# Attention with two feed-forward layers on one core: the half-filled query tile weighed by the full array, and the cosine's turn count written by ScalarE

## The chip, the cores and the metric

The kernel runs on one core of a Trainium2 chip. The metric is the device time of one execution in microseconds (us). The core has TensorE (PE; PEld is its weight load), VectorE (DVE), ScalarE (ACT), GpSimd (POOL) and SyncE (SP), whose queue here issues all transfers.

## What is computed

Attention over 4 batches and 8 heads with queries pooled in pairs (576 queries, 1152 keys, 64 wide), then two feed-forward layers over the 2304 rows; the first has the activation h·cos(h), the second silu.

```python
q_pool = q.reshape(B, H, S // factor, factor, D).mean(axis=3)
scores = scale * np.matmul(q_pool, k.transpose(0, 1, 3, 2))
attn = np.exp(scores - np.max(scores, axis=-1, keepdims=True))
attn = attn / (np.sum(attn, axis=-1, keepdims=True) + 1e-09)
x = np.matmul(attn, v)                    # heads side by side: 2304 x 512
h = x @ moe_w_in                          # 512 x 2048
x = (h * np.cos(h)) @ moe_w_out           # 2048 x 512
h = x @ moe2_w_in
out = (h * (1.0 / (1.0 + np.exp(-h)))) @ moe2_w_out
```

## The kernel before

All matmuls run in float16 pairs (a high and a low part of each number), three products for one.

**Attention.** Heads are taken in 16 pairs (4 batches, 4 pairs each). A pair has 576 queries per head, which make four full tiles of 128 queries for either head and one shared tile: 64 queries of the first head in its upper half, 64 of the second in its lower half. So there are nine tiles a pair and 144 in all. A tile goes through `tile_scores` (TensorE into PSUM), `tile_exp` (VectorE scales and finds the maximum, L409 and L414; ScalarE takes the exponential, L417), `tile_hi` (ScalarE, L423), `tile_lo` (GpSimd, L428, then a transposing transfer into `hlT`) and, four tiles later, `tile_pv` (L442), where the transposed weights are the stationary operand and the values move: 27 matmuls of 65 or 64 columns. For the shared tile `tile_pv` runs 27 matmuls on the first 64 stationary columns with the first head's values, and then 27 on the other 64 columns with the second head's values, each into its own 64 partitions of one slot of `pv`. `group_end` divides up to five tiles at a time on VectorE (L451 to L461).

**First layer.** The rows go through in nine blocks of 256 (two a batch, and one of all the shared tiles' rows). A block has 16 units `g1_unit` (L518, 12 matmuls of 256 columns each); two units fill a PSUM tile `h`, of which there are two. `g1_evac` (L531) copies two units to `hk`, scaled to turns. Every four units make a group of 128x1024: VectorE adds a quarter and a large constant (L543), takes the constant and `hk` off again (L544), which leaves the rounded turn count less the turns, ScalarE takes the sine (L550), VectorE multiplies (L553) and rounds to float16 (L558), GpSimd forms the low part (L559), and TensorE uses the result in `g2_unit1` (L578). The buffer `tt` of a group has two copies, shared with the block's result `y32` (L585 to L590), which is written to DRAM. There are 36 groups.

**Order.** First-layer units are handed out between the attention tiles (`share`), and a scheduler with priorities sets each engine's order when the program is built; the first layer's matmuls, the scores and the weighing of values therefore come interleaved in TensorE's queue, often one by one. The second layer's weights are decoded on VectorE, ScalarE and GpSimd (L206 to L240) after the last attention pair is loaded. The second layer (L518, L599) follows when the first is done.

Of the kernel before, what the change touches and what calls it, by code (L numbers as in the profile page):

```python
# [11 lines left out]
F32 = mybir.dt.float32  # L12
F16 = mybir.dt.float16
I32 = mybir.dt.int32
AF = mybir.ActivationFunctionType
ALU = mybir.AluOpType
# [5 lines left out]
MAGIC = 12582912.0  # L22
# [14 lines left out]
NB_HK, NB_TT, NB_G, SIN_N = 2, 2, 2, 2  # L37
# [3 lines left out]
GT = 5  # L41
# [3 lines left out]
def attention_moe_moe_kernel(ctx, tc, q, k, v, w_in1, w_out1, w_in2, w_out2, out):  # L45
# [3 lines left out]
    nc = tc.nc  # L49
    B, H, S, D = q.shape  # L50
# [6 lines left out]
    NT = SQ // 128  # L57
# [3 lines left out]
    const = ctx.enter_context(tc.tile_pool(name="const", bufs=1))  # L61
    wpool = ctx.enter_context(tc.tile_pool(name="w1", bufs=1))
    small = ctx.enter_context(tc.tile_pool(name="small", bufs=2))
# [3 lines left out]

    mean = const.tile([128, 128], F32, name="mean")
    halfpi = const.tile([128, 1], F32, name="halfpi")

    def make_consts():
        nc.vector.memset(mean, 2.0**-7)
        nc.vector.memset(halfpi, math.pi / 2)

    GW = 256

# [36 lines left out]
    @contextmanager  # L113
    def ahead(n):

        at_ = tc.cur_priority
        tc.cur_priority = at_ - n
        yield
        tc.cur_priority = at_ + (tc.cur_priority - (at_ - n))
# [147 lines left out]
    def att_pools(stack):  # L267
        at = Weights()
        at.p = stack.enter_context(tc.tile_pool(name="att", bufs=2, side="right", reuse_waits="tile"))
        at.src_stack = ExitStack()  # L270
        at.src = at.src_stack.enter_context(tc.tile_pool(name="src", bufs=2, side="right", reuse_waits="tile"))
        at.ps_s = stack.enter_context(tc.tile_pool(name="ps_s", bufs=1, space=PSUM, side="right"))
        at.ps_v = stack.enter_context(tc.tile_pool(name="ps_v", bufs=1, space=PSUM, side="right"))
        return at
# [102 lines left out]
    def tile_scores(at, P, t):  # L377


        T = Pair()  # L380
        T.P, T.t = P, t

        parts = [(0, 512), (512, S)]
        T.sp = [(a, z, at.ps_s.tile([128, z - a], F32, tag="sp%d" % a, name="sp")) for a, z in parts]
        if t < 2 * NT:
            kT = P.kT[t // NT]
            for a, z, sp in T.sp:
                for o, n in segs:
                    for e in range(2 if a <= o < z else 0):
                        nc.tensor.matmul(  # L390
                            sp[:, o - a:o - a + n], P.qT[e][:, t, :], kT[:, o:o + n], start=(e == 0), stop=(e == 1)
                        )
        else:
            for a, z, sp in T.sp:
                for o, n in segs:
                    for e in range(2 if a <= o < z else 0):
                        for i in range(2):
                            nc.tensor.matmul(
                                sp[i * 64:(i + 1) * 64, o - a:o - a + n], P.qT[e][:, t, i * 64:(i + 1) * 64],
                                P.kT[i][:, o:o + n], start=(e == 0), stop=(e == 1),  # L400
                            )
        return T
# [31 lines left out]
    def tile_pv(at, T):  # L434
        P, t, G = T.P, T.t, T.G
        if T.gi == 0:
            G.pv = at.ps_v.tile([128, GT, D + 1], F32, tag="pv", name="pv")
        hs = [(slice(0, 128), t // NT)] if t < 2 * NT else [(slice(0, 64), 0), (slice(64, 128), 1)]
        for r, i in hs:
            for c in range(KC):  # L440
                for e, z, n in ((0, 0, D + 1), (0, 1, D), (1, 0, D + 1)):
                    nc.tensor.matmul(  # L442
                        G.pv[r, T.gi, 0:n], T.hlT[:, e, c, r], P.vt[i][:, c, z, 0:n],
                        start=(c == 0 and e == 0 and z == 0), stop=(c == KC - 1 and e == 1),
                        skip_group_check=True,
                    )

    def group_end(at, G, n, dsts):

        den = small.tile([128, GT, 1], F32, tag="den", name="den", bufs=2)  # L450
        nc.vector.tensor_scalar(  # L451
            out=den[:, 0:n], in0=G.pv[:, 0:n, D:D + 1], scalar1=1e-9 * 2.0**PSH, scalar2=G.P.s[:, 2:3],
            op0=ALU.add, op1=ALU.mult,
        )
        nc.vector.reciprocal(den[:, 0:n], den[:, 0:n])
        for o, shape, dst in dsts:
            k = math.prod(shape)
            src, d = G.pv[:, o:o + k, 0:D], den[:, o:o + k].to_broadcast([128, k, D])
            if len(shape) == 2:
                src, d = (x.rearrange("p (t a) d -> p t a d", a=shape[1]) for x in (src, d))  # L460
            nc.vector.tensor_tensor(out=dst, in0=src, in1=d, op=ALU.mult)  # L461
# [62 lines left out]
    def g1_evac(mp, w, blk, f, first):  # L524
        if f % 2 == 0:
            return
        g = f * w.npc // NF
        if f % 4 == 1:
            blk.hk = mp.p.tile([128, 4, GW], F32, tag="hk", name="hk", bufs=NB_HK)
        o = blk.hk[:, (f % 4) - 1:(f % 4) + 1, :]  # L530
        nc.scalar.activation(  # L531
            out=o, in_=blk.hp, func=AF.Copy if first else AF.Silu, scale=blk.c.a[:, g:g + 1]
        )

    def g_cos_begin(mp, blk):

        G = Block()
        G.hk, G.K = blk.hk, blk.c.k
        G.gh = mp.p.tile([128, 4, GW], F16, tag="gh", name="gh", bufs=NB_G)
        G.gl = mp.p.tile([128, 4, GW], F16, tag="gl", name="gl", bufs=NB_G)  # L540
        blk.g.append((G.gh, G.gl))
        G.t = t = mp.p.tile([128, 4, GW], F32, tag="tt", name="tt", bufs=NB_TT)
        nc.vector.tensor_scalar(out=t, in0=G.hk, scalar1=0.25, scalar2=MAGIC, op0=ALU.add, op1=ALU.add)  # L543
        nc.vector.scalar_tensor_tensor(out=t, in0=t, scalar=MAGIC, in1=G.hk, op0=ALU.subtract, op1=ALU.subtract)  # L544
        return G

    def g_cos_end(groups):
# [68 lines left out]
    if True:  # L616
# [3 lines left out]
        xrem = wpool.tile([128, B, NP * D], F32, name="xrem")  # L620

        att_stack = ExitStack()
        at = att_pools(att_stack)
        wst_stack = ExitStack()
        wst = wst_stack.enter_context(tc.tile_pool(name="wst", bufs=1, reuse_waits="tile"))
        moe_stack = ExitStack()
        make_consts()

        state = Weights()
# [13 lines left out]
        def finish(g):  # L643
            while g in bg:
                advance()
# [45 lines left out]
        P = {}  # L691
# [36 lines left out]
        def x_of(b, i):  # L728
            if (b, i) not in x32:
                if (b - 1, i) in xgens:  # L730
                    finish(xgens[b - 1, i])
                x32[b, i] = wpool.tile([128, 2, DM], F32, tag="x32_%d" % i, name="x32")
            return x32[b, i]

        def block_done(b, i):
            if state.mp is None:
                finish(wg)
                wst_stack.close()
                state.mp = moe_pools(moe_stack)
            xgens[b, i] = block_steps(b, i)  # L740
            bg.append(xgens[b, i])

        def drain_pv():
            T = inflight.pop(0)
            G = T.G
            with ahead(P_PV):
                tile_pv(at, T)
            if T.gi < len(G.tiles) - 1:
                return
            b, j = T.P.b, T.P.j  # L750
            dsts = []
            if j < NP - 1:
                h = j + (G.tiles[0] // NT) * NP
                for i in range(2):
                    dsts.append((2 * i, (2,), x_of(b, i)[:, :, h * D:(h + 1) * D]))
            else:
                x = x_of(b, G.tiles[0] % NT // 2).rearrange("p t (a h d) -> p t a h d", a=2, d=D)
                dsts.append((0, (2, 2), x[:, :, :, j, :]))
            if G.tiles[-1] == 2 * NT:
                dsts.append((len(G.tiles) - 1, (1,), xrem[:, b:b + 1, j * D:(j + 1) * D]))  # L760
            group_end(at, G, len(G.tiles), dsts)
            if j == NP - 1:
                left[b] = left.get(b, set(range(2 * NT))) - set(G.tiles)
                for i in range(2):
                    if (b, i) not in gone and all(t % NT // 2 != i for t in left[b]):
                        gone.add((b, i))
                        block_done(b, i)
# [3 lines left out]
        for n, (b, j) in enumerate(pairs):  # L771
# [7 lines left out]
            for o in range(0, len(seq), GT):  # L779
                G = Pair()  # L780
# [9 lines left out]
            for idx, (G, gi, t) in enumerate(order):  # L790
                with ahead(P_SC):
                    T = tile_scores(at, P[n], t)
# [14 lines left out]
        while inflight:  # L807
            drain_pv()
            share(1)
# [23 lines left out]
        for i in range(2):  # L833
            T = wpool.tile([128, B, 2, 128], F16, tag="x32_%d" % i, name="xrT")
# [68 lines left out]
        for n in range(NB):  # L903
            nyb = y_load(n + 1) if n + 1 < NB else None
            gen = y_split(nyb) if nyb else None
            for f in range(NF):
# [7 lines left out]
                if len(pend) > 8:  # L914
                    blk, ff, nn = pend.pop(0)
# [43 lines left out]
```

## Time and profile before

| | us |
|---|---|
| median of three runs | 1435.6 (1434.48 to 1436.16) |
| profiled execution, its own time | 1439.78 |
| its span | 1438.0 |
| PE busy in the span | 1189.1 (83%) |
| DVE busy | 992.8 (69%) |
| ACT busy | 736.7 (51%) |
| POOL busy | 561.3 (39%) |

Busy time is an average over stages that differ: up to about 300 us there is attention alone with the decoding of the first layer's weights, up to about 888 us attention and first layer together, up to about 1037 us the rest of the first layer with the decoding of the second layer's weights, and from there on the second layer. In the rows, `128*64` is the part of the array that a matmul uses (rows by columns), `x22` is a count, and what stands behind `<-` in brackets is what ended an idle time.

### The profile page before, as it was taken

What the parts mean: (1) busy time and instruction counts of PE and PEld (TensorE: products, weight loads), DVE (VectorE), ACT (ScalarE), POOL (GpSimd) and SP (SyncE); (2) the same over time, 40 slices, a digit from 0 to 9 for tenths busy, and PEclk for the clock granted to TensorE, in tenths of its full rate; (3) what the DMA queues carried; (4) which work ended last, traced back from release to release, by engine and by line L of the source; (5) the groups of instructions that cost most, each with busy time, mean ns of one, the idle gap of its engine ahead of it and who ended that gap; (6) DMA issues with size and microseconds to landing.
All of it is one profiled execution on the core that took longest, in us unless ns stands there. A gap on an engine that the chain in (4) does not pass through costs nothing. (4 is left out here: it accounts for less than half of the span.)

```text
span 1438.0 us, 27552 instructions
## 1 busy us (share of the span) xinstructions
PE 1189.1 (83%) x11460; PEld 870.2 (61%) x11460; DVE 992.8 (69%) x1840; ACT 736.7 (51%) x763; POOL 561.3 (39%) x264
## 2 busy tenths in 40 slices
PE   1455365779988877998979989898899999999998
PEld 0233244566766655676656768777786666666665
DVE  7999987598787867987798895999833222323212
ACT  3676486477667667776667665546511111111110
POOL 1578375454556474656645552545410000000000
PEclk9986568798999998999999999989899999999999
DMA  7799889986799999997997965434210000000001
GB/s 230 191 232 199 206 161 187 207 159 111 153 210 164 198 204 185 202 162 161 182 188 144 222 102 107 123 113 132 74 60 30 15 16 30 30 30 15 16 1 30
DMA packets 493085, 186.34 MB, mean 130 GB/s; under 512 B 433056, under 2 KB 467872, under 8 KB 492960
## 3 DMA queue, kind: packets, MB, share of 16 engines
q1 hardware_dynamic: 492960, 184.59, 62.5%
q8 instruction: 89, 1.46, 0.4%
q14 instruction: 36, 0.29, 0.1%
HBM read 66.58 MB, written 9.44 MB: 53 GB/s over the span
## 5 line engine op out<-in xcount | busy, mean ns | idle before, releaser
L428 POOL TENSOR_TENSOR hl<-sc,hl 128x1152 f16<-128x1152 f32 x144 | 368.0, 2564 | 221.9 <-ACT hl L423 132.6
L442 PE MATMUL pv<-vt,hlT 128*128 128x65 f16 (+3 forms) x4320 | 253.5, 206 | 61.6 <-DMA hlT<-hl 45.2
L442 PEld LDWEIGHTS <-hlT 128*128 128x128 f16 (+1 forms) x4320 | 208.2, 108 | 119.0 <-DMA hlT<-hl 57.3
L518 PEld LDWEIGHTS <-ih 128*128 128x128 f16 x2304 | 226.4, 99 | 75.1 <-issue 14.9
L390 PE MATMUL sp<-kT,qT 128*128 128x512 f16 (+1 forms) x768 | 193.0, 366 | 95.1 <-DVE sc L409 77.7
L409 DVE TENSOR_SCALAR_CACHE_REDUCE sc<-sp,psu 128x512 f32<-128x512 f32 (+1 forms) x288 | 229.9, 808 | 52.1 <-PE sp L390 43.3
L531 ACT ACTIVATE hk<-h,ca 128x512 f32<-128x512 f32 x144 | 98.2, 683 | 326.8 <-PE h L518 326.8
L417 ACT ACTIVATE sc<-sc,nb 128x1152 f32<-128x1152 f32 x144 | 179.8, 1251 | 152.2 <-DVE nb L414 129.0
L518 PE MATMUL h<-ys,ih 128*128 128x256 f16 x1152 | 197.4, 274 | 2.9 <-ACT hk L531 2.9
L518 PE MATMUL h<-xT,ih 128*128 128x256 f16 x1024 | 190.6, 278 | 7.9 <-DVE pu__2739 L98 3.4
L423 ACT ACTIVATE hl<-sc 128x1152 f16<-128x1152 f32 x144 | 165.6, 1157 | 19.3 <-DMA hlT<-hl 11.7
L566 DVE TENSOR_SCALAR gh<-hk,ck 128x1024 f16<-128x1024 f32 x36 | 27.0, 751 | 206.9 <-PE o L599 194.2
L390 PEld LDWEIGHTS <-qT 128*128 128x128 f16 x768 | 76.3, 108 | 153.3 <-issue 112.3
L578 PE MATMUL y<-gh,oh 128*128 128x256 f16 x576 | 162.4, 282 | 4.2 <-ACT y L587 4.2
L578 PE MATMUL y<-gl,oh 128*128 128x256 f16 x576 | 162.2, 282 | 0.0
L578 PE MATMUL y<-gh,ol 128*128 128x256 f16 x576 | 162.0, 281 | 0.0
L518 PE MATMUL h<-ys,il 128*128 128x256 f16 x576 | 157.6, 274 | 0.0
L518 PE MATMUL h<-xT,il 128*128 128x256 f16 x512 | 142.7, 279 | 0.0
L559 POOL TENSOR_TENSOR gl<-tt,gh 128x1024 f16<-128x1024 f32 x36 | 87.6, 2434 | 112.7 <-DVE gh L558 82.3
L578 PEld LDWEIGHTS <-oh 128*128 128x128 f16 x1152 | 115.2, 101 | 23.8 <-issue 4.7
L518 PEld LDWEIGHTS <-il 128*128 128x128 f16 x1152 | 114.2, 99 | 18.9 <-issue 1.4
L599 PE MATMUL o<-ol,gh 128*128 128x512 f16 x288 | 109.1, 379 | 0.0
(279 smaller groups left out, 1776.6 us busy)
## 6 DMA issues: line engine op xcount, KB each, us to landing
wst<-in_moe_w_in_dram SPq DMA_DIRECT2D x16, 1024.0 KB, 6.1
wst<-in_moe_w_out_dram SPq DMA_DIRECT2D x16, 1024.0 KB, 6.1
stk<-in_k_dram SPq DMA_DIRECT2D x32, 288.0 KB, 4.1
stv<-in_v_dram SPq DMA_DIRECT2D x32, 288.0 KB, 4.1
stq<-in_q_dram SPq DMA_DIRECT2D x32, 256.0 KB, 3.2
ydr<-y SPq DMA_DIRECT2D x9, 512.0 KB, 2.6
y32b<-ydr SPq DMA_DIRECT2D x9, 512.0 KB, 3.2
out_dram<-osb SPq DMA_DIRECT2D x16, 256.0 KB, 2.1
```

What stands on the lines that cost most here:

```text
L390: nc.tensor.matmul(sp[:, o - a:o - a + n], P.qT[e][:, t, :], kT[:, o:o + n], start=(e == 0), stop=(e == 1))
L409: nc.vector.tensor_scalar(out=T.sc[:, a:z], in0=sp, scalar1=T.P.su, scalar2=None, op0=ALU.mult, op1=ALU.min, accum_out=mx[:, x:x + 1],)
L417: nc.scalar.activation(out=T.sc, in_=T.sc, func=AF.Exp, scale=-1.0, bias=nb)
L423: nc.scalar.activation(out=hi, in_=T.sc, func=AF.Copy)
L428: nc.gpsimd.tensor_tensor(out=T.hl[:, 1, :], in0=T.sc, in1=T.hl[:, 0, :], op=ALU.subtract)
L442: nc.tensor.matmul(G.pv[r, T.gi, 0:n], T.hlT[:, e, c, r], P.vt[i][:, c, z, 0:n], start=(c == 0 and e == 0 and z == 0), stop=(c == KC - 1 a ...
L518: nc.tensor.matmul(hp, wt[:, c, f * 128:(f + 1) * 128], xt(c), start=(i == 0), stop=(i == 3 * NC - 1), skip_group_check=True,)
L531: nc.scalar.activation(out=o, in_=blk.hp, func=AF.Copy if first else AF.Silu, scale=blk.c.a[:, g:g + 1])
L559: nc.gpsimd.tensor_tensor(out=G.gl, in0=t, in1=gh, op=ALU.subtract)
L566: nc.vector.tensor_scalar(out=gh, in0=hk, scalar1=blk.c.k, scalar2=None, op0=ALU.mult)
L578: nc.tensor.matmul(blk.y[:, oc, :], wt[:, f, oc * 128:(oc + 1) * 128], gt[:, f % 4, :], start=(f == 0 and e == 0 and oc % 2 == 0), stop=(f ...
L599: nc.tensor.matmul(blk.y[i], gt[:, f % 4, i * 128:(i + 1) * 128], wt[:, f, :], start=(f == 0 and e == 0), stop=(f == NF - 1 and e == 2),)
```

## The change

Two things are changed. The shared tile's weights are loaded whole (128 columns) in `tile_pv`, once with the first head's values and once with the second's, into two slots of `pv` of 128 partitions each, of which only the fitting half is divided and kept; `pv` and `den` get a sixth slot, and `group_end` writes the two halves apart. And in the first layer ScalarE reads each PSUM tile `h` a second time and writes turns plus a quarter into `tt` as 32-bit integers, with a bias of 0.25 from a 128x1 tile; VectorE's pass L543 goes, and L544 becomes a subtraction of `hk` from the integers. `tt` is now taken when the group's first two units are evacuated, where it was taken after its fourth.

```diff
     def tile_pv(at, T):
...
-        hs = [(slice(0, 128), t // NT)] if t < 2 * NT else [(slice(0, 64), 0), (slice(64, 128), 1)]
-        for r, i in hs:
+        for x, i in enumerate([t // NT] if t < 2 * NT else [0, 1]):
             for c in range(KC):
                 for e, z, n in ((0, 0, D + 1), (0, 1, D), (1, 0, D + 1)):
                     nc.tensor.matmul(
-                        G.pv[r, T.gi, 0:n], T.hlT[:, e, c, r], P.vt[i][:, c, z, 0:n],
+                        G.pv[:, T.gi + x, 0:n], T.hlT[:, e, c], P.vt[i][:, c, z, 0:n],
...
     def g1_evac(mp, w, blk, f, first):
...
             blk.hk = mp.p.tile([128, 4, GW], F32, tag="hk", name="hk", bufs=NB_HK)
+            if first:
+                blk.tt = mp.p.tile([128, 4, GW], F32, tag="tt", name="tt", bufs=NB_TT)
...
+        if first:
+            nc.scalar.activation(
+                out=blk.tt.bitcast(I32)[:, (f % 4) - 1:(f % 4) + 1, :], in_=blk.hp, func=AF.Identity,
+                scale=blk.c.a[:, g:g + 1], bias=quarter,
+            )
...
-        G.t = t = mp.p.tile([128, 4, GW], F32, tag="tt", name="tt", bufs=NB_TT)
-        nc.vector.tensor_scalar(out=t, in0=G.hk, scalar1=0.25, scalar2=MAGIC, op0=ALU.add, op1=ALU.add)
-        nc.vector.scalar_tensor_tensor(out=t, in0=t, scalar=MAGIC, in1=G.hk, op0=ALU.subtract, op1=ALU.subtract)
+        G.t = t = blk.tt
+        nc.vector.tensor_tensor(out=t, in0=t.bitcast(I32), in1=G.hk, op=ALU.subtract)
...
             if G.tiles[-1] == 2 * NT:
-                dsts.append((len(G.tiles) - 1, (1,), xrem[:, b:b + 1, j * D:(j + 1) * D]))
+                for i in range(2):
+                    r = slice(i * 64, (i + 1) * 64)
+                    dsts.append((len(G.tiles) - 1 + i, (1,), xrem[r, b:b + 1, j * D:(j + 1) * D], r))
```

The first place where the issued order matters is TensorE, in the weighing of a shared tile of the second batch (`hlT_3679` before, `hlT_3692` after). Before:

```order
L442 LDWEIGHTS hlT_3679
L442 MATMUL pv_3701<-vt_3030,hlT_3679 64x64
L578 LDWEIGHTS ol1_84
L578 MATMUL y_3121<-gh_3354,ol1_84 128x256
L442 LDWEIGHTS hlT_3679
L442 MATMUL pv_3701<-vt_3030,hlT_3679 64x65
L578 LDWEIGHTS oh1_83
L578 MATMUL y_3121<-gh_3354,oh1_83 128x256
```

And with the change:

```order
L443 LDWEIGHTS hlT_3692
L443 MATMUL pv_3713<-vt_3040,hlT_3692 128x65
L586 LDWEIGHTS ol1_85
L586 MATMUL y_3130<-gh_3367,ol1_85 128x256
L443 LDWEIGHTS hlT_3692
L443 MATMUL pv_3713<-vt_3040,hlT_3692 128x65
L586 LDWEIGHTS oh1_84
L586 MATMUL y_3130<-gh_3367,oh1_84 128x256
```

The one-by-one interleaving with the first layer stays; the weighing matmuls have 128 output partitions where they had 64. Over the program the shared tiles' weighing stood in 160 runs between other matmuls and now stands in 142.

The second place is ScalarE at the end of a first-layer block, after the attention (the group of `hk_12096` before, of `hk_12141` after; `y32` is the previous block's result). Before:

```order
L531 ACTIVATE hk_12096<-h_12045,ca_11466 128x512
L550 ACTIVATE tt_12017<-tt_12017,halfpi_73 128x1024
L238 ACTIVATE ih2_11530<-wst_11629,si2_112 128x4x256
L587 ACTIVATE y32_12037<-y_11281,cy_8678 128x256 x3
L206 ACTIVATE wt_11875<-wst_11775 128x1024
L587 ACTIVATE y32_12037<-y_11281,cy_8678 128x256
L831 ACTIVATE xnr_11523<-xrem_94,srem_11498 128x1024
L531 ACTIVATE hk_12096<-h_12117,ca_11466 128x512
```

And with the change:

```order
L535 ACTIVATE hk_12141<-h_12090,ca_11509 128x512
L595 ACTIVATE y32_12082<-y_11322,cy_8708 128x256 x4
L240 ACTIVATE ih2_11573<-wst_11671,si2_114 128x4x256
L841 ACTIVATE xnr_11566<-xrem_95,srem_11541 128x1024
L535 ACTIVATE hk_12141<-h_12164,ca_11509 128x512
L241 ACTIVATE wst_11671<-wst_11671,si2_114 128x1024
L208 ACTIVATE wt_11919<-wst_11818 128x1024
L539 ACTIVATE tt_12142<-h_12090,quarter_74,ca_11509 128x512
L539 ACTIVATE tt_12142<-h_12164,quarter_74,ca_11509 128x512
```

Both PSUM tiles `h` of the group are now read a second time at the end of this piece, behind the previous block's `y32` and two weight steps; before, each was free after its one reading.

## Rows read from the trace of the kernel before

**Rows 1.** Windows: span us, busy us of each engine (instructions), PEclk, DMA share, GB/s.
```profile
300.00:888.00 588.00, 505.80 (x5971) 383.57 (x5969) 479.54 (x948) 403.13 (x404) 328.47 (x155) 0.95 0.93 172
888.00:1037.00 149.00, 132.04 (x1112) 112.80 (x1110) 139.98 (x198) 85.38 (x94) 68.23 (x26) 0.93 0.37 107
1037.00:1438.00 401.00, 395.84 (x2776) 271.61 (x2774) 115.39 (x160) 64.03 (x91) 6.37 (x3) 0.99 0.08 26
```
**Rows 2.** Chain that ended last, in order of time: start us, us, what.
```profile
1013.57 2.38 DVE tt L543
...
1040.88 4.15 PE y L578 x38
```
**Rows 3.** Waits of TensorE and VectorE, 300 to 888 us: us in total, times, longest.
```profile
PE sp L390 <- DVE sc L409: 45.8, 33, 4.3
...
DVE sc L409 <- PE sp L390: 31.8, 30, 4.5
DVE den L451 <- PE pv L442: 14.7, 4, 5.4
```
**Rows 4.** Timeline of TensorE, a shared tile: start us, us, engine, line, operation, count.
```profile
816.07 0.22 PE L442 MATMUL pv<-vt,hlT 128*64 128x65 f16 x1
816.22 0.28 PE L578 MATMUL y<-gh,ol 128*128 128x256 f16 x1
816.43 0.22 PE L442 MATMUL pv<-vt,hlT 128*64 128x65 f16 x1
```
**Rows 5.** Timeline of TensorE, a full tile in the same interleaving.
```profile
601.60 0.19 PE L442 MATMUL pv<-vt,hlT 128*128 128x64 f16 x1
601.62 0.28 PE L578 MATMUL y<-gl,oh 128*128 128x256 f16 x1
601.74 0.19 PE L442 MATMUL pv<-vt,hlT 128*128 128x65 f16 x1
```
**Rows 6.** Timeline of TensorE: first and last half-width run of 300 to 888 us.
```profile
317.90 0.41 PE L442 MATMUL pv<-vt,hlT 128*64 128x65 f16 x7
...
865.15 1.46 PE L442 MATMUL pv<-vt,hlT 128*64 128x65 f16 x43
```
**Rows 7.** Timeline of TensorE: a long run of full width.
```profile
541.70 0.84 PE L442 MATMUL pv<-vt,hlT 128*128 128x65 f16 x22
```
**Rows 8.** Groups by line: out<-in, shapes, count, busy us, mean ns, idle before.
```profile
L417 ACT ACTIVATE sc<-sc,nb 128x1152 f32<-128x1152 f32 x144 | 179.8, 1251 | 152.2 <-DVE nb L414 129.0 <-DVE ui L106 5.2 <-DVE si L102 5.0
L423 ACT ACTIVATE hl<-sc 128x1152 f16<-128x1152 f32 x144 | 165.6, 1157 | 19.3 <-DMA hlT<-hl 11.7 <-DMA xT<-xn 4.8 <-POOL hl L428 0.7
L531 ACT ACTIVATE hk<-h,ca 128x512 f32<-128x512 f32 x144 | 98.2, 683 | 326.8 <-PE h L518 326.8
L553 DVE SCALAR_TENSOR_TENSOR tt<-hk,ck,tt 128x1024 f32<-128x1024 f32 x36 | 67.2, 1868 | 17.3 <-ACT tt L550 17.2
L544 DVE SCALAR_TENSOR_TENSOR tt<-tt,hk 128x1024 f32<-128x1024 f32 x36 | 58.6, 1629 | 0.2
L543 DVE TENSOR_SCALAR tt<-hk 128x1024 f32<-128x1024 f32 x36 | 40.3, 1120 | 14.2 <-ACT hk L531 10.4 <-DMA ydr<-y 3.6 <-POOL gl L559 0.2
L461 DVE TENSOR_TENSOR xrem<-pv,den 128x64 f32<-128x64 f32 x16 | 3.4, 213 | 0.0
```
**Rows 9.** Windows of line L543 alone: span us, DVE busy us (count).
```profile
300.00:888.00 588.00, 25.88 (x23) 0.95 0.93 172
888.00:1037.00 149.00, 12.65 (x11) 0.93 0.37 107
```
**Rows 10.** Timeline of ScalarE, GpSimd and SyncE at two first-layer groups of the rest stage.
```profile
928.64 0.66 ACT L531 ACTIVATE hk<-h,ca 128x512 f32<-128x512 f32 x1
...
937.72 2.13 POOL L559 TENSOR_TENSOR gl<-tt,gh 128x1024 f16<-128x1024 f32 x1 [4.77 <-DVE ui L98]
...
1029.48 0.68 ACT L531 ACTIVATE hk<-h,ca 128x512 f32<-128x512 f32 x1
...
1038.22 0.34 SPq L590 DMA_DIRECT2D ydr<-y  x1
```

More of the change, by code (lines that the diff above doesn't have):

```diff
@@ L69, in attention_moe_moe_kernel @@
     halfpi = const.tile([128, 1], F32, name="halfpi")
+    quarter = const.tile([128, 1], F32, name="quarter")
     def make_consts():
@@ L73, in make_consts @@
         nc.vector.memset(halfpi, math.pi / 2)
+        nc.vector.memset(quarter, 0.25)
     GW = 256
@@ L436, in tile_pv @@
         if T.gi == 0:
-            G.pv = at.ps_v.tile([128, GT, D + 1], F32, tag="pv", name="pv")
-        hs = [(slice(0, 128), t // NT)] if t < 2 * NT else [(slice(0, 64), 0), (slice(64, 128), 1)]
-        for r, i in hs:
+            G.pv = at.ps_v.tile([128, GT + 1, D + 1], F32, tag="pv", name="pv")
+        for x, i in enumerate([t // NT] if t < 2 * NT else [0, 1]):
             for c in range(KC):
@@ L448, in group_end @@
     def group_end(at, G, n, dsts):
-        den = small.tile([128, GT, 1], F32, tag="den", name="den", bufs=2)
+        n += G.tiles[-1] == 2 * NT
+        den = small.tile([128, GT + 1, 1], F32, tag="den", name="den", bufs=2)
         nc.vector.tensor_scalar(
@@ L455, in group_end @@
         nc.vector.reciprocal(den[:, 0:n], den[:, 0:n])
-        for o, shape, dst in dsts:
+        for o, shape, dst, r in dsts:
             k = math.prod(shape)
-            src, d = G.pv[:, o:o + k, 0:D], den[:, o:o + k].to_broadcast([128, k, D])
+            src, d = G.pv[r, o:o + k, 0:D], den[r, o:o + k].to_broadcast([r.stop - r.start, k, D])
             if len(shape) == 2:
@@ L754, in drain_pv @@
                 for i in range(2):
-                    dsts.append((2 * i, (2,), x_of(b, i)[:, :, h * D:(h + 1) * D]))
+                    dsts.append((2 * i, (2,), x_of(b, i)[:, :, h * D:(h + 1) * D], slice(0, 128)))
             else:
                 x = x_of(b, G.tiles[0] % NT // 2).rearrange("p t (a h d) -> p t a h d", a=2, d=D)
-                dsts.append((0, (2, 2), x[:, :, :, j, :]))
+                dsts.append((0, (2, 2), x[:, :, :, j, :], slice(0, 128)))
             if G.tiles[-1] == 2 * NT:
-                dsts.append((len(G.tiles) - 1, (1,), xrem[:, b:b + 1, j * D:(j + 1) * D]))
+                for i in range(2):
+                    r = slice(i * 64, (i + 1) * 64)
+                    dsts.append((len(G.tiles) - 1 + i, (1,), xrem[r, b:b + 1, j * D:(j + 1) * D], r))
             group_end(at, G, len(G.tiles), dsts)
```

## The prediction
> **What bounds the kernel now.** I read the windows by stage first, then the chain that ended last, then who waits for whom in the mixed stage, and last TensorE's timeline inside a shared tile. The windows [rows 1] split what the average hides. From 1037 us on TensorE is busy for 396 of 401 us at a granted clock of 0.99: this is the second layer, the change touches nothing in it, and a gain must bring its start forward. The chain [rows 2] confirms it: at 1040.88 us it is TensorE's, and at 1013.57 us one of VectorE's steps in the cosine holds it for 2.38 us. In the rest stage (888 to 1037 us) VectorE is busy for 140 of 149 us, ScalarE for 85 [rows 1]. In the mixed stage (300 to 888 us) nothing is full: TensorE 506, VectorE 480, ScalarE 403 of 588 us, and the transfers have a share of 0.93 [rows 1]. There TensorE and VectorE wait for each other [rows 3]: TensorE 45.8 us for the scores to be taken out of PSUM, VectorE 31.8 us for scores and 14.7 us for weighed values. Time taken from either counts where the other is waiting for it.
>
> TensorE's busy time hides something that only start times show. In a shared tile the half-width weighing alternates with first-layer matmuls [rows 4]: 816.07, 816.22, 816.43, so one pair takes 0.36 us. A full tile in the same alternation starts at 601.60, 601.62, 601.74 [rows 5]: 0.14 us a pair. So passing from the full array to half of it and back costs 0.22 us, while no engine is waited for. In unbroken runs the halves are not slower: 43 matmuls of half width take 1.46 us [rows 6], 22 of full width 0.84 us [rows 7]; less the 0.19 us of the last one [rows 5] that is 30 and 31 ns from start to start.
>
> **Part one, the shared tile.** The matmul count stays (54 a shared tile), and so does their pace (30 against 31 ns, taken as nothing). The passages go. Between 300 and 888 us I count 159 half-width runs in TensorE's timeline, 121 of them a single matmul; the first and the last run stand in [rows 6]. All of them at 0.22 us give 35 us, the single ones alone 27 us. I take 32 us, near the upper end, since the long runs have two ends as well and only some of these fall into a wait. The passages into and out of the shared tile's scores stay, as that code is unchanged.
>
> Of the 32 us not all shortens the stage. TensorE waits for VectorE or a transfer in roughly 14% of it (588 less 506 us), which would allow up to 0.86; on the other side VectorE's 46 us of waiting for TensorE are about half of what the two wait for each other (46 against 46), which gives 0.5. I take 0.6, close to the lower one, since the transfers at 0.93 leave less room: **19 us**. The bounds are 0 (another engine sets the pace) and 35 us.
>
> The Trainium skill has a rule against this part: in "TensorEngine Tiling (Array Packing)", section Key Properties, different tiles of a divided array load and multiply in parallel, so that the two halves of a shared tile could run side by side and the change would give that up. The trace does not show it, the 30 ns of [rows 6] being the pace of one matmul after the other. By the rule 27 matmuls in each of the stage's twelve shared tiles would come on top, 12 x 27 x 0.03 = 10 us, and the gain of this part would be (32 - 10) x 0.6 = 13 us.
>
> `group_end` gets one more small division per pair: 16 x 0.21 us = 3.4 us by [rows 8], on VectorE. It is hidden behind the 26 us that the second part takes from VectorE in the mixed stage; without that cover, 2 us.
>
> **Part two, the turn counts.** VectorE loses L543: 36 x 1.12 us = 40.3 us [rows 8], of which 25.9 us lie in the mixed stage and 12.7 us in the rest stage [rows 9]. L544 becomes a two-tensor subtraction with an integer operand, which the trace does not have; the nearest row is L544 itself at 1.63 us, and I take that. The bounds are L543 at 1.12 us and L553 at 1.87 us [rows 8], so 36 x 0.51 = 18 us less to 36 x 0.24 = 9 us more on VectorE.
>
> ScalarE gains 72 instructions of 128x512 from PSUM. The evacuation L531 of this shape takes 0.683 us [rows 8]; a bias operand costs some 0.09 us more if I compare the exponential L417 (1.251 us, with bias) to the copy L423 (1.157 us, without) [rows 8]. I take 0.777 us, the upper end, since the new one has a bias: 56 us in all, some 36 us of it in the mixed stage (twice the 23 groups) and 17 us in the rest stage (twice 11). ScalarE has 185 and 64 us free there [rows 1], so I cost it at nothing; if that cover were gone it would be these 36 and 17 us.
>
> What VectorE loses in the mixed stage I don't add to part one: VectorE's waits for TensorE are counted there, and it is the same exchange. It supports the 0.6. In the rest stage VectorE is the bound at 140 of 149 us, and L543 stands on the chain, once with 2.38 us [rows 2]. Of the 12.7 us I take 0.4, **5 us**, since the sine between L544 and L553 stands on ScalarE, behind its added 17 us, and TensorE too is busy for 132 us. The bounds are 12.7 us, and below zero the second rival.
>
> **Sum.** 19 + 5 = 24 us off the profiled execution's 1439.8 us is 1415.8 us. That execution lies 4.2 us above the median of the runs, 1435.6 us, so I predict 1411.6, **1412 us**. As a case of its own this reaches from 1400 to 1425 us.
>
> **Rivals.**
>
> *Another pace.* In the mixed stage the transfers' share of 0.93 is near full [rows 1], and ScalarE goes from 403 to about 439 of 588 us. If one of these sets the tile's pace, part one gives little. Against it speaks that TensorE's longest waits are for VectorE [rows 3]. Then only the 5 us of the rest stage and a few more are left: **1431 us**, 1427 to 1438. ScalarE's share in this is what a rule of the skill points to: "ScalarE: Activation LUTs", section Rules for kernel authors, wants plain adds and multiplies on VectorE. By the rows it is 56 us on ScalarE for 40 us on VectorE, dearer in sum, but on the engine with more time free.
>
> *Slower: `tt` taken too early.* `tt` has two copies and is now needed when a group's first half leaves PSUM. At 928.64 us the first half of a group is evacuated, while the copy that it would need is free only when GpSimd ends at 937.72 + 2.13 = 939.85 us [rows 10]: 11 us late. In the last such group the copy is held by the previous block's `y32`, whose transfer is only issued at 1038.22 us where the first half left PSUM at 1029.48 us [rows 10]: 9 us and the transfer. I matched every group of the rest stage in this way and found five of about 10 to 12 us, some 54 us in sum; these two are the second and the last. Until then the PSUM tile `h` is held, with two such tiles TensorE stops, and whatever is queued behind the write on ScalarE stands. Before, the wait was VectorE's and came two units later. If half of the 54 us lands on the chain, the rest stage costs 27 us more, and if the same waits take back a third of the mixed stage's 19 us, 13 us stay: 1435.6 + 27 - 13 = **1450 us**. The point of decision is at 13 us, a quarter of the 54. Against it speaks that VectorE, not the first layer's evacuation, is late there (140 of 149 us), so that much of it is time in which nobody needs `h`.
>
> *All of it.* If both savings land whole, 35 + 12.7 = 48 us: **1388 us**. For it speaks that TensorE and VectorE, who wait for each other, are both relieved.
>
> That the change doesn't do what it says I leave without a chance of its own: the interleaving stays in the issued order (142 runs for 160), so the passages are there to be saved.
>
> **Chances.** Forecast 0.53, another pace 0.19 (half of it within 0.2%), slower 0.13, all of it 0.15. What a measurement of this kernel can tell from no change is about 0.2%, 3 us. So faster 0.78, same 0.09, slower 0.13. The range goes from **1390 us** (half of "all of it" left out) to **1438 us** (which leaves out the slower case).
>
> **What would show it.** Right: a shared tile's alternation in TensorE's timeline at 0.14 us a pair, no `128*64` rows on the weighing line, the mixed stage shorter by some 20 us with TensorE's waits for VectorE about as before; 72 ScalarE instructions near 0.78 us; the rest stage shorter by about 5 us with VectorE still the busiest. Wrong: `tt` writes on ScalarE that stand for GpSimd or the `y32` transfer for more than 20 us in sum and TensorE waiting for ScalarE before L518; a mixed stage as long as before with TensorE waiting more; or full-width matmuls slower than 31 ns from start to start.

## The result, and the profile after

The change takes 1415.8 us in the median of four runs (1412.5 to 1418.3), against 1435.0 us for the kernel before in the same comparison: a ratio of 0.9867, 95% interval 0.9837 to 0.9897, or 19.2 us less. The forecast was 1412 us, faster. The profiled execution took 1418.3 us, 21.5 us less than that of before.

These are the windows of the changed kernel, with the same columns as [rows 1]. I set the limits by the same events: the mixed stage ends 4 us ahead of the seventh first-layer block's first evacuation, and the last stage begins within about a microsecond of where TensorE's unbroken chain begins.

```profile
300.00:865.00 565.00, 477.94 (x5983) 376.71 (x5982) 463.04 (x922) 432.55 (x447) 325.75 (x156) 0.94 0.97 179
865.00:1008.00 143.00, 119.32 (x1021) 102.34 (x1019) 125.90 (x191) 94.72 (x108) 64.20 (x25) 0.95 0.40 111
1008.00:1416.50 408.50, 403.39 (x2848) 278.48 (x2846) 123.06 (x165) 69.49 (x97) 8.48 (x4) 1.00 0.07 25
```

The mixed stage is 23 us shorter, the rest stage 6 us, and the last stage 7.5 us **longer**, although nothing in the second layer's code was changed. So the net gain is the mixed stage's, and behind it nothing is gained. What moved there can be seen in TensorE's timeline, first in the kernel before, around the end of the first layer:

```profile
1036.79 0.58 PE L518 MATMUL h<-ys,ih 128*128 128x256 f16 x2 [2.87 <-ACT hk L531]
...
1061.57 0.27 PE L578 MATMUL y<-gh,ol 128*128 128x256 f16 x1
1061.68 0.38 PE L518 MATMUL h<-ys,ih 128*128 128x256 f16 x2
```

and now in the changed kernel (the first row is from its chain, in order of time):

```profile
1014.19 20.96 PE y L586 x192
...
1034.88 0.27 PE L586 MATMUL y<-gh,ol 128*128 128x256 f16 x1
1034.99 0.38 PE L520 MATMUL h<-ys,ih 128*128 128x256 f16 x2
```

`h<-ys` are second-layer matmuls. Before, 48 of them start ahead of the first layer's last `y`, some at 1036.79 us; in the change none does, though their input `ys` was written from 870.7 us on. At 0.109 us each (192 in 20.96 us) that is 5.2 us of work that TensorE did ahead of the last `y` and now does behind it. From the last `y` to the end it is accordingly 376.4 us before and 381.6 us in the change.

Not all of the 48 had filled a gap. The first 24 start from 1031.14 us on, and behind them TensorE stands idle for 2.87 us (the bracket of the first row above). The other 24 come after that wait, and the chain of before runs through them, ahead of the last block's `y`:

```profile
1036.79 4.09 PE h L518 x24
```

So what TensorE is seen to have done in its spare time is the first 24, 2.6 us.

I therefore compare the kernels below by three pieces of about equal work: **A**, the time of the first evacuation of the first layer's seventh block; **B**, from there to the last `y` matmul; **C**, from there to the end. A stands in these two rows of ScalarE's timeline, before and after:

```profile
892.24 0.69 ACT L531 ACTIVATE hk<-h,ca 128x512 f32<-128x512 f32 x1 [1.42 <-PE h L518]
```
```profile
869.42 0.69 ACT L535 ACTIVATE hk<-h,ca 128x512 f32<-128x512 f32 x1 [2.89 <-PE h L520]
```

The waits of TensorE and VectorE in the mixed stage of the change (300 to 865 us; in total, times, longest) stand beside [rows 3]:

```profile
PE sp L392 <- DVE sc L411: 43.3, 32, 3.7
PE pv L443 <- DMA hlT<-hl: 19.8, 13, 2.7
...
DVE sc L411 <- PE sp L392: 25.3, 23, 3.1
DVE pm L113 <- DMA stk<-in_k_dram: 24.7, 9, 4.7
...
DVE den L453 <- PE pv L443: 0.7, 1, 0.7
```

TensorE waits for VectorE about as long as before. VectorE waits 6.5 us less for the scores, and its 14.7 us of waiting for weighed values have shrunk to 0.7 us. What is late next is the keys' load (11.9 us before, 24.7 us now). The groups of the lines that the change touches stand beside [rows 8]:

```profile
L561 DVE SCALAR_TENSOR_TENSOR tt<-hk,ck,tt 128x1024 f32<-128x1024 f32 x36 | 74.3, 2064 | 14.8 <-ACT tt L558 14.8
L552 DVE TENSOR_TENSOR tt<-tt,hk 128x1024 f32<-128x1024 int32 x36 | 60.5, 1679 | 16.0 <-ACT tt L539 16.0
L539 ACT ACTIVATE tt<-h,quarter,ca 128x512 int32<-128x512 f32 x72 | 55.1, 770 | 11.1 <-DMA ydr<-y 11.0
L463 DVE TENSOR_TENSOR xrem<-pv,den 64x64 f32<-64x64 f32 x32 | 6.9, 216 | 0.2
```

This is a shared tile of the changed kernel in TensorE's timeline, beside [rows 4]:

```profile
743.65 0.19 PE L443 MATMUL pv<-vt,hlT 128*128 128x64 f16 x1
743.68 0.27 PE L586 MATMUL y<-gl,oh 128*128 128x256 f16 x1
743.79 0.19 PE L443 MATMUL pv<-vt,hlT 128*128 128x65 f16 x1
```

A pair takes 0.14 us, where it took 0.36.

### The profile page after: what moved, and what is told of

It reads as the page before. It is cut to its first block, busy times and chain, and to the rows that moved or that the text cites. A ratio compares the mean times of both kernels' runs of the same rounds, so it can differ in the third digit from the quotient of the medians.

```text
span 1416.5 us, 27577 instructions
## 1 busy us (share of the span) xinstructions
PE 1155.1 (82%) x11460; PEld 859.3 (61%) x11460; DVE 968.8 (68%) x1821; ACT 783.5 (55%) x833; POOL 555.1 (39%) x264
## 5 line engine op out<-in xcount | busy, mean ns | idle before, releaser
L430 POOL TENSOR_TENSOR hl<-sc,hl 128x1152 f16<-128x1152 f32 x144 | 364.3, 2538 | 203.8 <-ACT hl L425 140.3
L443 PE MATMUL pv<-vt,hlT 128*128 128x65 f16 (+1 forms) x4320 | 243.3, 205 | 66.2 <-DMA hlT<-hl 50.9
L392 PE MATMUL sp<-kT,qT 128*128 128x512 f16 (+1 forms) x768 | 197.2, 374 | 99.3 <-DVE sc L411 74.8
L443 PEld LDWEIGHTS <-hlT 128*128 128x128 f16 x4320 | 208.9, 106 | 104.6 <-DMA hlT<-hl 62.0
L520 PE MATMUL h<-xT,ih 128*128 128x256 f16 x1024 | 185.8, 276 | 6.4 <-ACT tt L539 2.2
```

The lines of the kernel that those rows point to most:

```text
L392: nc.tensor.matmul(sp[:, o - a:o - a + n], P.qT[e][:, t, :], kT[:, o:o + n], start=(e == 0), stop=(e == 1))
L430: nc.gpsimd.tensor_tensor(out=T.hl[:, 1, :], in0=T.sc, in1=T.hl[:, 0, :], op=ALU.subtract)
L443: nc.tensor.matmul(G.pv[:, T.gi + x, 0:n], T.hlT[:, e, c], P.vt[i][:, c, z, 0:n], start=(c == 0 and e == 0 and z == 0), stop=(c == KC - 1 ...
L520: nc.tensor.matmul(hp, wt[:, c, f * 128:(f + 1) * 128], xt(c), start=(i == 0), stop=(i == 3 * NC - 1), skip_group_check=True,)
```

## The experiments

Every ratio is to the kernel before, run beside it (median 1437 to 1439 us there); the change has its own comparison, so that kernels are set against it by these ratios. Gains in us are the ratio's distance times 1437. The pieces A, B and C of each kernel (us) are worked out from the start times in its trace, of one profiled execution each. Such an execution can lie some microseconds from the median of its kernel's runs (before 4.2 us above it, e1 2.9 us below, e11 5.9 us above), so a difference of a few microseconds between two pieces says little by itself.

| kernel | ratio (95%) | A | B | C |
|---|---|---|---|---|
| before | 1 | 892.2 | 169.3 | 376.4 |
| the change | 0.9867 (0.9837–0.9897) | 869.4 | 165.5 | 381.6 |
| e1 shared tile only | 0.9887 (0.9863–0.9911) | 871.7 | 168.1 | 376.4 |
| e2 turns only | 0.9926 (0.9901–0.9952) | 875.0 | 166.7 | 381.8 |
| e3 halves in turn | 0.9940 (0.9920–0.9961) | 881.6 | 166.3 | 379.1 |
| e4 turns written twice | 0.9907 (0.9878–0.9935) | 874.0 | 172.1 | 381.1 |
| e5 half width, unbroken | 0.9833 (0.9805–0.9861) | 866.2 | 168.4 | 376.4 |
| e6 weighed again | 0.9934 (0.9910–0.9957) | 875.5 | 165.0 | 381.7 |
| e7 idle pass | 0.9997 (0.9975–1.0018) | 885.4 | 171.2 | 381.7 |
| e8 result apart | 0.9877 (0.9852–0.9903) | 870.4 | 162.5 | 382.0 |
| e9 unbroken and turns | 0.9835 (0.9811–0.9860) | 861.5 | 166.4 | 381.7 |
| e10 full width, unbroken, turns | 0.9799 (0.9773–0.9824) | 861.5 | 167.0 | 381.7 |
| e11 dead write | 1.0016 (0.9993–1.0040) | 892.4 | 169.4 | 380.3 |
| e12 split division | 0.9980 (0.9961–0.9999) | 887.3 | 169.0 | 376.4 |

**e1, part one alone.** Part two is taken out of the change again:

```diff
...
-        G.t = t = blk.tt
-        nc.vector.tensor_tensor(out=t, in0=t.bitcast(I32), in1=G.hk, op=ALU.subtract)
+        G.t = t = mp.p.tile([128, 4, GW], F32, tag="tt", name="tt", bufs=NB_TT)
+        nc.vector.tensor_scalar(out=t, in0=G.hk, scalar1=0.25, scalar2=MAGIC, op0=ALU.add, op1=ALU.add)
+        nc.vector.scalar_tensor_tensor(out=t, in0=t, scalar=MAGIC, in1=G.hk, op0=ALU.subtract, op1=ALU.subtract)
```

> The first part alone: the shared tile weighed by the full array, VectorE's rounding pass L543 kept. My theory (the passages between full and half array are TensorE time on the path): 13 to 20 us faster than before, 1415 to 1422 us, with the whole gain in the mixed stage (attention and first layer together), no alternation slower than 0.14 us a pair, and a rest stage as long as before. Rival (VectorE sets the mixed stage's pace, and the gain comes from the 26 us taken from it there): 0 to 5 us faster, 1430 to 1435 us, TensorE's waits for VectorE longer by about what the passages saved.

It gave 16 us (13 to 20), all of it in A (20.5 us in the profile). The one-by-one alternation with the first layer stays here, so what is gone is the passages, while the matmuls are twice as wide.

**e2, part two alone.** `tile_pv` and `group_end` as before, the other edits as in the change:

```diff
-        for x, i in enumerate([t // NT] if t < 2 * NT else [0, 1]):
+        hs = [(slice(0, 128), t // NT)] if t < 2 * NT else [(slice(0, 64), 0), (slice(64, 128), 1)]
+        for r, i in hs:
```

> The second part alone: ScalarE writes the turn counts, the shared tile still weighed by halves. My theory: 2 to 7 us faster than before, 1428 to 1433 us, the gain in the rest stage, where VectorE is the busiest. Rival (VectorE sets the mixed stage's pace): 13 to 20 us faster, 1415 to 1422 us, with the mixed stage shorter. Second rival (the turn buffer is taken too early): slower than before, over 1440 us, ScalarE standing over 20 us in sum before its integer writes.

It gave 10.6 us (7 to 14), more than I had expected, and in another place: in A it is 17.2 us, where I had looked for it in the rest stage; B gives 2.6 and C takes 5.4. So part two does work in the mixed stage, and does not add to part one: 20.5 and 17.2 alone, 22.8 together in A; 16 and 10.6 alone, 19 together by the ratios. Behind A it is a loss of 2.8 us. The half-width matmuls stand in 147 runs here for 160, so that some 2 us of the gain can be passages (13 at 0.22 us and 0.6).

**e3, the halves in turn.** The kernel before, in which the two halves' matmuls alternate, so that both halves of the array have work at a time; as many passages between widths as before (160 runs).

```diff
-        for r, i in hs:
-            for c in range(KC):
-                for e, z, n in ((0, 0, D + 1), (0, 1, D), (1, 0, D + 1)):
+        for c in range(KC):
+            for e, z, n in ((0, 0, D + 1), (0, 1, D), (1, 0, D + 1)):
+                for r, i in hs:
```

> The kernel before with the two halves of a shared tile weighed in turn, matmul by matmul, where it did 27 of the one and then 27 of the other. If different halves of the array work side by side in this use, as the scores of the shared tile do in the trace (3 to 4 ns from one start to the other), an unbroken run comes to some 15 to 17 ns a matmul, and the time falls by up to 10 us, 1425 to 1432 us. If they don't, the run stays at 30 ns a matmul and the time within 4 us of before, 1431 to 1439 us. In both cases the passages into and out of the half array stay, some 0.22 us a pair.

It gave 8.6 us (6 to 11). One row of TensorE's timeline shows the pace:

```profile
701.37 0.57 PE L442 MATMUL pv<-vt,hlT 128*64 128x65 f16 x24
```

24 matmuls in 0.57 us; less the 0.22 us of the last [rows 4] that is 15 ns from start to start, half of the 30 ns of [rows 6]. The halves do run side by side if they are issued in turn. The passages remain, and their removal in e1 gives about twice as much.

**e4, every integer write made twice**, to the same place, in the change:

```diff
-        if first:
+        for _ in range(2 if first else 0):
             nc.scalar.activation(
```

> The changed kernel with every integer write of ScalarE issued twice (the same values to the same place): 72 more instructions of 0.77 us, 55 us more on ScalarE, some 36 us of it in the mixed stage and 17 us in the rest stage. My theory (ScalarE has the time free): at most 6 us slower than the change, 1413 to 1422 us. Rival (ScalarE is on the path, so that the 55 us already added cost time): 15 to 40 us slower, 1431 to 1456 us.

It took 5.7 us more than the change by the ratios (0 to 12 by the two intervals). In the profile A is 4.6 us later and B 6.6 us longer. For 55 us more on ScalarE that is cheap, but probably not nothing, in the mixed stage and behind it.

**e5, half width but in one piece.** The kernel before with one number changed:

```diff
-            with ahead(P_PV):
+            with ahead(P_PV if T.t < 2 * NT else 300):
                 tile_pv(at, T)
```

> The kernel before with one number changed: the shared tile's weighing gets the highest priority, so that its 54 half-width matmuls stand in one piece in TensorE's queue (16 runs, no single ones, where 160 runs stood). No matmul, width or instruction changes. Theory (the passages between full and half array cost 0.22 us a pair and that is what part one saves): the short passages at the weighing vanish, and the time falls by as much as the shared tile alone gave, ratio to the kernel before 0.985 to 0.991. Rival (the gain of the shared tile came from the wider writes or from the changed order, not from the passages): 0.997 or above, and above 1.002 if pieces of 54 matmuls in a row, 1.6 us each, make scores or first-layer units late.

The highest priority goes to the shared tile's weighing, so that its 54 matmuls stand together in TensorE's queue. It gave 24 us (20 to 28), more than part one and than I had expected. Here is a shared tile in its timeline (the row's shape is that of its first matmul, a full-width one; the 54 behind it are of half width):

```profile
740.07 1.93 PE L442 MATMUL pv<-vt,hlT 128*128 128x65 f16 x55
741.93 0.28 PE L578 MATMUL y<-gl,oh 128*128 128x256 f16 x1
```

Between 300 and 888 us the start times of before show 303 passages between half and full width at the weighing, counted in and out one by one, that cost 35.0 us in sum (time to the next start less the median pace of matmuls of that shape, without the seven above 0.4 us); e5 has 21 of 2.0 us in sum. No matmul is wider here, so the gain does not need the width. But e5 changes two things: the passages are gone, and the tile is weighed at once, which is worth something by itself (e10 below). The price of the passages alone is therefore read from the start times and from e1, which takes them away and keeps the alternation. From the start of a shared tile's first matmul to the end of its last, the twelve tiles of the stage take 89.0 us in sum before, 58.6 us in the change, 22.6 us in e5 and 22.9 us in e10.

**e6, the shared tile weighed twice over**, full width, in the change:

```diff
-        for x, i in enumerate([t // NT] if t < 2 * NT else [0, 1]):
+        for x, i in [(0, t // NT)] if t < 2 * NT else [(0, 0), (1, 1)] * 2:
```

> The changed kernel, in which each shared tile is weighed twice over (the second time overwrites the first with the same values): 54 full-width matmuls more a shared tile, 16 x 54 x 0.031 us = 27 us of TensorE's time, 20 us of it in the mixed stage, and no passage between widths. This measures the factor by which TensorE's time in the mixed stage counts. Theory (0.6): 12 us more than the change, ratio to the kernel before 0.995 (0.992 to 0.998). Rival 1 (another engine sets the pace, factor 0): 0.987. Rival 2 (factor 1, TensorE alone sets the pace): 1.001 or above.

It took 9.6 us more than the change, 0.48 of the 20 us (0.2 to 0.75 by the two intervals). The factor of 0.6 lies in this, 0 and 1 do not. It is not a clean measure, though: the granted clock is higher in all seven executions of e6 (0.928 to 0.937) than in the change's four (0.921 to 0.927), and from 300 us to the end of A TensorE's busy time grew by 12.6 us only (482.4 to 495.0), not by 20. In that one execution A is 6.1 us later.

**e7, a pass that does nothing** is given back to VectorE, in the change:

```diff
         G.t = t = blk.tt
+        nc.vector.tensor_scalar(out=G.hk, in0=G.hk, scalar1=0.0, scalar2=0.0, op0=ALU.add, op1=ALU.add)
```

> The changed kernel, in which VectorE gets a pass of the same size back that does nothing (it adds zero to hk in place, ahead of the subtraction of hk): 36 x 1.12 us as L543 before, at the same place in the chain. ScalarE keeps its 72 writes. Theory (part two gains by VectorE's time): its gain is gone and what is left is part one, ratio to the kernel before 0.988 to 0.992. Rival 1 (part two gains by something else, say by the earlier turn counts): stays at 0.987. Rival 2 (ScalarE's 56 us cost something that VectorE's relief has covered): 0.993 or above.

The whole gain was gone, 18.7 us more than the change. The theory's number fell, the second rival's came, but its reason is not borne out at that size by e11 below. Two groups of VectorE's lines in e7 are

```profile
L562 DVE SCALAR_TENSOR_TENSOR tt<-hk,ck,tt 128x1024 f32<-128x1024 f32 x36 | 74.2, 2062 | 15.1 <-ACT tt L559 15.1
L553 DVE TENSOR_TENSOR tt<-tt,hk 128x1024 f32<-128x1024 int32 x36 | 66.7, 1854 | 1.2 <-ACT tt L539 0.4 <-issue 0.3 <-DVE hk L552 0.2
```

and the same two steps in e1, which has the same passes on VectorE:

```profile
L544 DVE SCALAR_TENSOR_TENSOR tt<-tt,hk 128x1024 f32<-128x1024 f32 x36 | 62.5, 1735 | 0.1
L553 DVE SCALAR_TENSOR_TENSOR tt<-hk,ck,tt 128x1024 f32<-128x1024 f32 x36 | 62.3, 1729 | 17.3 <-ACT tt L550 17.2
```

VectorE needs 36 x 0.33 = 12.0 us more for the same multiplications and 36 x 0.12 = 4.3 us more for the subtractions. In the multiplications it meets GpSimd longer (the last section): by the trace GpSimd is at work during 1.08 us of one of them in e7, 0.74 us in e1. For the subtractions it is 1.01 and 1.07 us, so that their 4.3 us are not explained by this. Of e7's 16 us over e1, 5.3 us lie in C, as no second-layer matmul stands ahead of the last `y` in e7 and 48 do in e1. How much of the rest is VectorE's longer steps, and how much the earlier hold on `tt`, stays open.

**e8, `y32` out of the ring of `tt`**, in the change:

```diff
-        y32 = mp.p.tile([128, NC, GW], F32, tag="tt", name="y32", bufs=NB_TT)
         for oc in range(NC):
+            y32 = mp.p.tile([128, GW], F32, tag="yq", name="y32", bufs=2)
...
+            nc.sync.dma_start(out=ydst[:, oc * GW:(oc + 1) * GW], in_=y32)
```

> The changed kernel, in which the block's result y32 leaves the ring of the tt tiles: it goes through two tiles of its own of 1 KB a partition, in four transfers of 128 KB where one of 512 KB was. The integer writes then don't wait for that transfer (11.0 us of waiting in the change). Theory (these waits lie mostly beside VectorE's work, as the second rival failed): 0 to 4 us faster than the change, ratio to the kernel before 0.984 to 0.987. Rival (the tt rival, smaller than feared but there): 8 to 11 us faster, 0.979 to 0.981. Slower than the change if the four transfers and their issues disturb the transposing transfers: above 0.989.

The wait is gone, as the row of the integer writes shows (11.1 us of idle time in the change, 2.2 us here), and the time is that of the change (0.9877 to 0.9867, well within the intervals):

```profile
L539 ACT ACTIVATE tt<-h,quarter,ca 128x512 int32<-128x512 f32 x72 | 55.6, 772 | 2.2 <-POOL gl L567 2.2
```

**e9, e5's number together with part two**, half width (on e2):

```diff
-            with ahead(P_PV):
+            with ahead(P_PV if T.t < 2 * NT else 300):
```

> The unbroken half-width weighing together with part two of the change (ScalarE's integer writes, no VectorE pass), nothing of part one's full width. The question is whether this beats the change and the unbroken weighing alone (0.9833). If part two adds as it did behind the shared tile (change 0.9867 to shared tile alone 0.9887): ratio to the kernel before 0.979 to 0.983. If it adds as much as alone (0.9926): 0.974 to 0.978. Rival (ScalarE's writes eat what VectorE's relief gives, once the passages are gone): 0.983 to 0.987.

0.9835 to e5's 0.9833: the rival came. A is 4.6 us earlier than in e5, B and C together 3.3 us longer, and on the median nothing is left.

**e10, the change with e5's number**, full width:

```diff
-            with ahead(P_PV):
+            with ahead(P_PV if T.t < 2 * NT else 300):
```

> The changed kernel, full width and part two, with the shared tile's 54 matmuls in one piece by priority. Unbroken half width gave 0.9833 where the full width, interleaved, gave 0.9887; this tells apart why. Theory A (with full width there is no passage left to save, and the order is worth nothing): 0.985 to 0.989, as the change. Theory B (weighing the shared tile at once is worth some 8 us by itself, since its slot, and the group that ends with it, come free sooner): 0.979 to 0.983.

28.9 us less than before (25 to 33) and some 10 us less than the change: the lowest of all, though its interval overlaps with e5's. Theory B holds: where no passage is left to save, weighing the shared tile at once still gives something. Its twelve tiles take 1.8 to 2.9 us each, as in this row:

```profile
730.14 1.83 PE L443 MATMUL pv<-vt,hlT 128*128 128x65 f16 x54 [0.40 <-DMA hlT<-hl]
```

Whether full width is worth anything over half width once the tile is in one piece is not settled: A is 861.5 us in e9 and e10 alike, and the intervals of the two overlap. Nor is it shown why the shorter stretch helps; that the group's slots in PSUM are divided and freed sooner is my guess.

**e11, the second reading alone**: the kernel before, with a write that nobody reads.

```diff
...
+        if first:
+            dead = mp.p.tile([128, 2, GW], I32, tag="dead", name="dead", bufs=1)
+            nc.scalar.activation(
+                out=dead, in_=blk.hp, func=AF.Identity, scale=blk.c.a[:, g:g + 1], bias=quarter,
+            )
```

> The kernel before, in which ScalarE reads each first-layer PSUM tile a second time and writes the integers to a scratch tile that nobody reads; VectorE's two passes and the tt tiles stay as they were. 72 x 0.77 = 56 us on ScalarE alone, without VectorE's relief and without the earlier hold on tt. Theory of the prediction (ScalarE has the time free, cost nothing): ratio to the kernel before 1.000 to 1.002. Rival by the idle pass (with VectorE as loaded as before, the writes cost some 16 us, as that kernel stood 0.011 above the shared tile alone): 1.006 to 1.011. If it is the earlier hold on tt that cost there, this one shows nothing of it and stays below 1.003.

2 us more (1 us less to 6 more). In the profile A is unchanged (892.4 to 892.2 us) and C 3.9 us longer, with 23 second-layer matmuls ahead of the last `y` instead of 48. So the writes move 25 of these matmuls behind the last `y`, 2.7 us of work. Whether they are free in the mixed stage is not shown by this: in e11 the half-width matmuls also stand in 132 runs for 160, which by e12 below (131 runs) should give some 3 us, and the granted clock of its profiled mixed stage is 0.92 where it is 0.95 before. A price of a few us, as in e4's A, stays possible.

**e12, the split division alone**, the kernel before with the change's two pieces of 64 partitions in `group_end`:

```diff
...
-                dsts.append((len(G.tiles) - 1, (1,), xrem[:, b:b + 1, j * D:(j + 1) * D]))
+                for i in range(2):
+                    r = slice(i * 64, (i + 1) * 64)
+                    dsts.append((len(G.tiles) - 1, (1,), xrem[r, b:b + 1, j * D:(j + 1) * D], r))
```

> The kernel before with nothing but the changed group_end: the shared tile's division is made in two 64-partition pieces, 16 more instructions of 0.21 us on VectorE, 3.4 us in sum. It is also a control for what a mere change of the scheduler's order does: the half-width runs stand in 131 pieces for 160. Theory: 0 to 2 us more by VectorE, up to 4 us less by 29 passages fewer, ratio to the kernel before 0.997 to 1.002. Rival (the order alone moves the time by as much as the parts of the change do): outside 0.995 to 1.005.

3 us less (0 to 6). The added instructions cost nothing that can be seen; the 29 runs fewer, at the 0.22 us and 0.6 of the forecast, would be 3.8 us. As a control it is one case in which a mere change of the order moved the time by less than either part of the change did.

## Why the prediction was right, step by step

- **The passages.** 0.22 us a pair and 32 us in sum were right in size: 35.0 us over the matmuls' own pace by the start times, and none left at the weighing in the change. The count behind it was slightly high: the start times give 155 half-width runs and 120 single ones, for 159 and 121. With e1 for the passages without the order, and e5 for half width kept, they and not the width are the cost.
- **The factor of 0.6.** Not contradicted, but not measured closely either: e1's 16 us are half of 32 by the medians, its A of 20.5 us is 0.64; e6 gives 0.48 with other work of TensorE's, at a higher clock.
- **The rule against it** (the Trainium skill, "TensorEngine Tiling (Array Packing)", section Key Properties, that different tiles work in parallel). The trace of before did not show it since 27 matmuls of one half came ahead of 27 of the other; e3 shows it, at 15 ns for 30. So e3's trace agrees with the rule, and its giving up was no loss here, because the kernel before did not use it. The 13 us that I worked out by it lie at the edge of e1's interval.
- **`group_end`.** 6.9 us in all where it was 3.4 us, so the 3.4 us more came as priced; e12 shows no cost of it.
- **The subtraction from integers** at 1.63 us: 1.68 us. **The integer writes** at 0.777 us: 0.770 us. Both are right in size.
- **No sum over VectorE's relief and part one in the mixed stage.** Right: 20.5 and 17.2 us alone make 22.8 us. I had put 19 us there.
- **The rest stage's 5 us** is the step that failed. From A on, the change is 1.3 us slower than before. B is 3.8 us shorter, and VectorE is still the busiest in that stage (126 of 143 us), but C grew by 5.2 us: 48 matmuls of the second layer that stood ahead of the last `y` now stand behind it. The other profiles go the same way: C is 376.4 us with 48 ahead, 379.1 with 24 (e3), 380.3 with 23 (e11), 381.1 with 5 (e4), and 381.6 to 382.0 with none. The move could have been read in the order of TensorE's queue; I had written of the second layer that "the change touches nothing in it" without looking whether its first matmuls keep their place.
- **Why nothing was left of the 5 us** is not settled by that. Since 24 of the 48 had stood on the chain of B, for 4.09 us, part of B's 3.8 us can be their absence and not VectorE's relief. The relief itself does show in B, as far as single profiles can tell: with VectorE's pass given back and none of the 48 ahead (e7), B is 5.7 us longer than in the change. Against it stand ScalarE's writes, which I had put at nothing: a second set of them (e4) makes B 6.6 us longer. Whether putting the matmuls back gains the 5 us was not tried.
- **ScalarE at nothing.** Not confirmed: by e4 a second set costs 5.7 us (0 to 12), 4.6 us later in A and 6.6 us longer in B in its profile; e11 costs 2 us (1 less to 6 more), 3.9 us longer in C. What the change's own set costs is open, at a few us of the 53 us that I had named for the case without cover.
- **The sum.** 24 us forecast on the profiled execution, 21.5 us measured; the medians differ by 19.2 us. What is short is the rest stage's 5 us, partly made up by the mixed stage's 22.8 for 19: that the sum came out so near is in part luck.

Of the rivals, *another pace* fell with e1 and e5. *Slower* fell too: the integer writes did stand for `ydr`, but for 11.0 us in all, and without that wait (e8) nothing is gained. *All of it* fell too: the two parts give 16 and 10.6 us alone and 19 us together, far from 48; that they share one exchange between TensorE and VectorE is the reason I had given, and it fits.

## What to carry to other kernels

A matmul that uses half of the array costs nothing more by itself here, but every passage between half and full width does, some 0.1 us; where half-width work lies interleaved with other work, look at the start times (busy time hides it), and first try to put it in one piece, which gave more here (24 us) than making it full width (16 us). Two savings at both ends of one exchange did not add. And where a stage behind the change is counted as untouched, check in the order of the queue that the work which filled its gaps still stands ahead.

## What was not expected of the hardware

The mean of VectorE's multiplication rose from 1.87 to 2.06 us though nothing in it was changed. The single instructions of the change differ widely. Alone it takes 1.27 us:

```profile
897.72 1.27 DVE L561 SCALAR_TENSOR_TENSOR tt<-hk,ck,tt 128x1024 f32<-128x1024 f32 x1
```

Beside GpSimd it takes up to 3.40 us. In these two rows, which overlap, it is 3.19 us:

```profile
842.21 2.37 POOL L430 TENSOR_TENSOR hl<-sc,hl 128x1152 f16<-128x1152 f32 x1
...
842.47 3.19 DVE L561 SCALAR_TENSOR_TENSOR tt<-hk,ck,tt 128x1024 f32<-128x1024 f32 x1 [2.43 <-ACT tt L558]
```

GpSimd is done at 842.21 + 2.37 = 844.58 us, and VectorE 1.08 us later, at 845.66. Alone the step takes 1.27 us, so nearly all of it came after GpSimd's end. The other way round GpSimd waits, and its step of 2.13 us [rows 10] takes 2.99 us where VectorE began first:

```profile
919.66 1.23 DVE L552 TENSOR_TENSOR tt<-tt,hk 128x1024 f32<-128x1024 int32 x1
...
919.90 2.99 POOL L567 TENSOR_TENSOR gl<-tt,gh 128x1024 f16<-128x1024 f32 x1 [8.74 <-DVE gh L566]
```

The Trainium skill, "SBUF — State Buffer", section "SBUF: two separate sides", calls this an exclusive lock that the engine which starts first keeps for its whole instruction, for a VectorE step with two inputs in SBUF against a GpSimd step that reads it; these rows agree. So the mean durations of [rows 8] for the two-tensor steps, on which I had built bounds, depend on how often VectorE meets GpSimd: where no GpSimd instruction lies beside it, the old subtraction takes 1.21 to 1.23 us (eleven of its 36 in the kernel before), and so does the one from integers (eleven of 36 in the change).
